# Fewer operations in a 64-bit weight conversion, row gates on ScalarE, output weights split in pieces, and a last pair of products by row tiles

## The chip, the core and the metric

The kernel runs on one core of a Trainium2 chip. Five engines work side by side, each through its own instructions in order: TensorE (PE, matrix products), VectorE (DVE), ScalarE (ACT), GpSimd (POOL) and SyncE (SP, which issues most transfers). They meet through semaphores. The metric is the device time of one execution in microseconds (us), lower is better: here the median of three executions.

## The reference, cut to what matters

Three layers follow each other; the input is 4 batches of 768 positions, 8 heads of 64, so 3072 tokens of 512 numbers.

```python
x = attention(q, k, v)            # 8 global positions, a local window of 96, per-head distance bias
logits = x @ moe_w_gate;  e = argmax(logits);  gate = softmax(logits)[e]
y[t] = gate[t] * (relu(x[t] @ w1[e[t]]) @ w2[e[t]])        # 8 experts, 512 -> 1024 -> 512
out = (sigmoid(y @ w_gate) * (y @ w_val)) @ w_out          # 512 -> 1536 -> 512, weights are float64
```

The three weights of the last layer arrive as 64-bit floats; everything else is 32-bit. The output is 32-bit.

## The kernel before, in words

**Values split in two.** Products run in 16-bit floats at full rate. A 32-bit value becomes a high half (`wh`, `xh`, `hh`) and a low half, value minus high (`wl`, `xl`, `hl`), and a product becomes three: high-high, high-low, low-high. High halves are copies on ScalarE; low halves are subtractions on VectorE.

**Stage 1, to about 215 us: attention**, laid out by a planner. The change does not touch it.

**Stage 2, about 215 to 524 us: the experts** (`ffn`). Tokens are gathered by expert; the experts are ranked by load and make nine items with 256, 256, 480, 448, 416, 400, 384, 368 and 352 token columns. Each item has eight steps `f`, written out one after the other. In a step TensorE does the 12 products of `mm1` for the step to come (tile `hp`), and the 12 of `mm2` for this one (tiles `acc`). ScalarE makes `hh` from `hp`, VectorE makes `hl`. Beside that, a step prepares what comes later:

- `wsplit`: ScalarE's `wh` and VectorE's `wl` (128x1024) of the weights of the step to come;
- for `f` from 1 to 4, `xgate` on a gathered row tile of the next item: VectorE multiplies 128x512 numbers by the token's gate, one number per row (tile `xg`). Two steps later `xprep` turns `xg` on TensorE and splits it into `xT`. The row tile `x` came by GpSimd's indirect transfer;
- the class `Prep` converts the 64-bit weights in 36 pieces of 128x512, up to six pieces an item. `start` reads the two 32-bit words (`raw`): ScalarE takes the absolute value of the high word as a float (L926, `u`), VectorE shifts the low word (L927, `v`), scales and bounds `u` (L928), joins the two (L929), and puts the sign back (L936). A step later `finish` stores the result or, for the output weights, which come in pairs, forms four differences on GpSimd (L960). A step after that it splits the pair into 16-bit halves (`parts`): a block of 256 columns and one of 1536, each a copy on ScalarE (L946) and a subtraction on GpSimd (L947). One step later SyncE stores them (L950, memory `wz`). Six pairs are done so, one an item; the splits stand in the step `f` = 2 and the store in `f` = 3, one step later in the last of these items.

**Stage 3, about 524 to 1035 us: the gated layer** (`Gated`), in four chunks of 768 tokens. `first` makes the hidden values `h` by seven products in place of eight (sums and differences of blocks stand in for one product). `second` multiplies by the output weights, again seven products a chunk (numbers 0 to 6), each of 54 matmuls on 256 columns. For each, `hsplit` makes the two halves of a block of `h` (tile `wk`, two buffers), `hsum` the next sum of blocks, and `post` adds results to the output tiles `o`, whose rows are sent by GpSimd's indirect transfers (`scatter`, L1494). Every product has two of the eight PSUM banks: X is 6 and 7, Z 4 and 5, W 2 and 3, Y 0 and 1, in the order X, Z, X, W, Y, Z, W. Product 6 thus writes banks that `post` of 4 reads. In the last chunk product 6 goes row tile by row tile into banks 2, 3 and 0. Just ahead of it stand range checks and a `vote`, a 128x2 product on TensorE of VectorE's verdicts (`ok`), from which a flag chooses at the end whether a slower general path must run.

The order on each engine is the order in which the code is written; a tile waits for its buffer.

## Time and profile before

| | us |
|---|---|
| time, three runs | 1037.35, 1037.74, 1038.54; median 1037.74 |
| the profiled execution | 1036.72, of which span 1034.9 |
| attention, experts, gated layer | to about 215, to about 524, to the end |
| TensorE busy | 93% of the span, mean granted clock 0.986 of full |

A group of rows below is one view of this profiled execution: busy time by engine, waits by who was waited for, or the timeline of an engine, in which square brackets hold the idle time before an instruction and what ended it. Line numbers are those of the kernel above.

### The profile page before, as it was taken

How to read it: one execution, taken by the hardware profiler on the slowest of the kernel's cores; microseconds unless marked ns; L12 is line 12 of the kernel's file. 1: busy time of each engine (PE TensorE's matmuls, PEld its weight loads, DVE VectorE, ACT ScalarE, POOL GpSimd, SP SyncE). 2: the span in 40 equal slices, each digit the busy share in tenths (PEclk: the TensorE clock that was granted, in tenths of full speed). 3: DMA queues.
4: the chain of work that ended last, by engine and by line, in shares of the span. 5: the costliest groups of instructions: out<-in, count | busy, mean ns of one | idle time of the engine just before them, and what ended most of it. 6: DMA issues, size and time to landing. Idle time of an engine off the chain costs nothing. (4 is left out here: it accounts for less than half of the span.)

```text
span 1034.9 us, 21115 instructions
## 1 busy us (share of the span) xinstructions
PE 962.7 (93%) x7983; PEld 674.3 (65%) x7983; DVE 780.9 (75%) x1628; ACT 502.4 (49%) x960; POOL 443.5 (43%) x617
## 2 busy tenths in 40 slices
PE   6989887799999999998999999999999999999994
PEld 4778776678555555565555578666786668766684
DVE  5989988975789899988776789444884449744594
ACT  5989888743445545554644354212532226221340
POOL 7799988951412512423567840323112250222102
PEclk9999999989999999999999999999999999999998
DMA  9677676257887998896668646453164523554031
GB/s 198 165 183 181 160 166 144 75 169 239 257 295 252 309 310 269 296 317 222 177 204 284 217 146 235 166 200 133 62 230 172 204 98 118 209 201 175 1 123 65
DMA packets 165701, 197.35 MB, mean 191 GB/s; under 512 B 88547, under 2 KB 129910, under 8 KB 165590
## 3 DMA queue, kind: packets, MB, share of 16 engines
q1 hardware_dynamic: 159990, 181.73, 55.9%
q0 software_dynamic: 5008, 14.11, 4.1%
q8 instruction: 64, 1.05, 0.4%
q14 instruction: 47, 0.39, 0.1%
q10 hardware_dynamic: 592, 0.08, 0.1%
HBM read 146.81 MB, written 49.23 MB: 189 GB/s over the span
## 5 line engine op out<-in xcount | busy, mean ns | idle before, releaser
L1351 PE MATMUL q<-yo,set 128*128 128x384 f16 x2016 | 330.5, 326 | 2.1 <-DVE h L1398 1.8
L1351 PEld LDWEIGHTS <-set 128*128 128x128 f16 x2016 | 197.1, 98 | 134.3 <-issue 5.1
L1442 PE MATMUL p<-wy,wk 128*128 128x256 f16 x1458 | 160.5, 273 | 2.0 <-DVE wk L1338 2.0
L1442 PEld LDWEIGHTS <-wk 128*128 128x128 f16 x1512 | 147.5, 98 | 20.6 <-DVE wk L1338 3.1
L1121 PE MATMUL hp<-xT,wh 128*128 128x256 f16 (+7 forms) x576 | 135.9, 323 | 0.3
L1402 POOL TENSOR_TENSOR h<-h,t 128x384 f32<-128x384 f32 x60 | 59.0, 997 | 151.9 <-DVE t L1398 136.4
L1121 PE MATMUL hp<-xT,wl 128*128 128x256 f16 (+7 forms) x288 | 93.1, 323 | 9.4 <-DVE wl L1022 9.4
L1494 POOL DMA_INDIRECT out_dram<-o,idt x24 | 23.5, 980 | 181.5 <-DVE o L1458 174.1
L1022 DVE SCALAR_TENSOR_TENSOR wl<-wr,wh 128x1024 f16<-128x1024 f32 x64 | 95.3, 1490 | 7.1 <-ACT wh L1017 6.3
L1138 PE MATMUL acc<-hl,wh 128*128 128x256 f16 (+7 forms) x288 | 92.8, 322 | 5.6 <-DVE hl L1126 5.6
L1372 ACT ACTIVATE u<-q 128x384 f32<-128x384 f32 x48 | 23.1, 481 | 153.9 <-PE q L1351 153.9
L1138 PE MATMUL acc<-hh,wh 128*128 128x256 f16 (+7 forms) x288 | 93.0, 323 | 0.0
L1138 PE MATMUL acc<-hh,wl 128*128 128x256 f16 (+7 forms) x288 | 92.7, 322 | 0.0
L1036 POOL DMA_INDIRECT x<-xd,idx x29 | 33.1, 1140 | 129.9 <-DMA idx<-lst 123.2
L1404 ACT ACTIVATE h<-h 128x384 f32<-128x384 f32 x72 | 37.6, 522 | 102.3 <-DVE h L1398 72.5
L570 ACT ACTIVATE pp<-tt,mall 128x232 f32<-128x232 f32 (+1 forms) x192 | 81.5, 487 | 5.1 <-DVE mall L553 3.4
L1125 ACT ACTIVATE hh<-hp 128x256 f16<-128x256 f32 (+7 forms) x72 | 34.6, 480 | 99.2 <-PE hp L1121 97.8
L1138 PEld LDWEIGHTS <-wh 128*128 128x128 f16 x576 | 56.4, 98 | 35.2 <-issue 0.7
L1374 DVE TENSOR_TENSOR u<-q,u 128x384 f32<-128x384 f32 x48 | 26.8, 558 | 68.0 <-PE q L1351 68.0
L1121 PEld LDWEIGHTS <-wh 128*128 128x128 f16 x576 | 56.4, 98 | 31.3 <-ACT wh L1017 0.5
L553 DVE CUSTOM_DVE_ANT_0 tt<-s,nb 128x232 f32<-128x232 f32 (+1 forms) x192 | 64.5, 365 | 0.3 <-PE s L541 0.3
L1017 ACT ACTIVATE wh<-wr 128x1024 f16<-128x1024 f32 x60 | 62.9, 1049 | 3.1 <-DMA wr<-in_moe_w_dram 3.1
(214 smaller groups left out, 1929.9 us busy)
## 6 DMA issues: line engine op xcount, KB each, us to landing
wr<-in_moe_w_dram SPq DMA_DIRECT2D x64, 512.0 KB, 5.7
set<-us SPq DMA_DIRECT2D x36, 896.0 KB, 4.8
wy<-wz SPq DMA_DIRECT2D x28, 768.0 KB, 4.4
us<-set SPq DMA_DIRECT2D x12, 896.0 KB, 6.1
kn<-in_k_dram SPq DMA_DIRECT2D x24, 256.0 KB, 4.9
qn<-in_q_dram SPq DMA_DIRECT2D x24, 256.0 KB, 5.3
vn<-in_v_dram SPq DMA_DIRECT2D x24, 256.0 KB, 4.7
raw<-in_moe_w_gate_dram SPq DMA_DIRECT2D x12, 512.0 KB, 5.7
```

What stands on the lines that cost most here:

```text
L553: nc.vector.tensor_tensor_reduce(out=tt[s][:, j, :w], in0=S_[s][j % 2][:, j // 2, :w], in1=g.nb[w][:, h, :], scale=-0.125 / (QSC * QSC), s ...
L570: nc.scalar.activation(pp[s][:, j, 256 - w :], tt[s][:, j, :w], AF.Exp, bias=g.mall[:, t, h : h + 1], scale=-1.0)
L1017: self.tc.nc.scalar.activation(hi, raw, AF.Copy, scale=WS[z])
L1022: self.tc.nc.vector.scalar_tensor_tensor(lo, self.raws.pop((z, p)), WS[z], hi, op0=ALU.mult, op1=ALU.subtract)
L1036: self.tc.nc.gpsimd.indirect_dma_start(out=x, out_offset=None, in_=self.g.xd[0:n], in_offset=bass.IndirectOffsetOnAxis(ap=self.idx[i][:, j ...
L1121: nc.tensor.matmul(bk, a[:, k, fs], b[:, k, :], start=(m == 0), stop=(m == 11))
L1125: nc.scalar.activation(hh, bk, AF.Relu)
L1138: nc.tensor.matmul(acc[i][dk], a[:, f % 2, d], b, start=(f == 0 and m == 0), stop=(f == NF - 1 and m == 2))
L1351: nc.tensor.matmul(bk, w[:, za, a, us], self.y[zy][:, y, u, :], start=(start and n == 0), stop=(n == 5), skip_group_check=not start,)
L1402: (V if last else G).tensor_tensor(at(half, tok), at(half, tok), d, op=ALU.mult)
L1404: A.activation(d, d, AF.Sigmoid, scale=1.0 / (YS * AS[0]))
L1442: nc.tensor.matmul(bks[t], w[:, za, j, 128 * t : 128 * t + 128], y[:, j, zy, :], start=(new and j == 0 and m == 0 and (end or t != 1)), st ...
```

## The change

- The bound on small numbers goes from the conversion, and the scale moves into ScalarE's absolute value, so L928 has no successor; shift and join stay, with another join (`or`).
- `xgate` runs on ScalarE for all items but the first: 27 of 29 tiles.
- The pair's split comes in four pieces, 256, 512, 512 and 512 columns, one a step, at `f` = 2 to 5, with the store at `f` = 6; in the last of these items at 3 to 6 and 7.
- `wk` has three buffers. In `second`'s loop the next `hsplit` and `hsum` now stand ahead of `post`.
- In the last chunk products 5 and 6 go together, row tile by row tile (`close`), into the banks 4 and 2, 5 and 3, 6 and 0; results are added and scattered tile by tile. The vote is cut in three: verdicts after the second of the six groups, the product ahead of the fifth, the flag after it.

```diff
 KEPT = (0, 2, 3, 4, 5, 6, 7)
-W64MIN = float(1.125 * 2.0 ** -15)
+EXP8 = 2.0 ** -112
...
@@ -923,10 +923,9 @@
         u = g.cv.tile([128, 512], U32, tag="u", name="u", bufs=3)
         v = g.cv.tile([128, 512], U32, tag="v", name="v", bufs=1)
         uf = u.bitcast(F32)
-        nc.scalar.activation(uf, hi.bitcast(F32), AF.Abs)
-        nc.vector.tensor_scalar(v, lo, 29, 0x80000000, op0=ALU.logical_shift_right, op1=ALU.bitwise_or)
-        nc.vector.tensor_scalar(uf, uf, W64MIN, 2.0 ** -16 * (OX if m == 2 else 1.0), op0=ALU.max, op1=ALU.mult)
-        nc.vector.scalar_tensor_tensor(u, u, 3, v, op0=ALU.logical_shift_left, op1=ALU.bitwise_xor)
+        nc.scalar.activation(uf, hi.bitcast(F32), AF.Abs, scale=EXP8 * (OX if m == 2 else 1.0))
+        nc.vector.tensor_single_scalar(v, lo, 29, op=ALU.logical_shift_right)
+        nc.vector.scalar_tensor_tensor(u, u, 3, v, op0=ALU.logical_shift_left, op1=ALU.bitwise_or)
         if m == 2:
             if f < NJ:
                 self.pair = g.cv.tile([128, 8, 256], U32, tag="pair", name="pair", bufs=2)
@@ -939,15 +938,7 @@
     def finish(self):
         g, nc = self.g, self.tc.nc
         if self.late:
-            j, x, z = self.late.pop(0)
-            if z is None:
-                z = g.cv.tile([128, len(KEPT), 2, 256], F16, tag="parts", name="parts", bufs=2)
-                for o, b, k in ((0, 0, 1), (1, 2, 6)):
-                    nc.scalar.activation(z[:, o : o + k, 0, :], x[:, b : b + k, :], AF.Copy)
-                    nc.gpsimd.tensor_tensor(z[:, o : o + k, 1, :], x[:, b : b + k, :], z[:, o : o + k, 0, :], op=ALU.subtract)
-                self.late.append((j, x, z))
-            else:
-                nc.sync.dma_start(out=g.wz[:, :, j].rearrange("b p z c -> p b (z c)"), in_=z.rearrange("p b z c -> p b (z c)"))
+            self.late.pop(0)()
         if self.half is None:
             return
         f, m, uf = self.half
@@ -958,7 +949,19 @@
             x = self.pair.bitcast(F32)
             for o, a, b in ((4, 1, 0), (6, 3, 1), (5, 3, 4), (7, 2, 5)):
                 nc.gpsimd.tensor_tensor(x[:, o, :], x[:, a, :], x[:, b, :], op=ALU.subtract)
-            self.late.append((f - NJ, x, None))
+            z = g.cv.tile([128, len(KEPT), 2, 256], F16, tag="parts", name="parts", bufs=2)
+            def split(o, b, k):
+                hi, lo = (z[:, o : o + k, y, :] for y in range(2))
+                nc.scalar.activation(hi, x[:, b : b + k, :], AF.Copy)
+                nc.gpsimd.tensor_tensor(lo, x[:, b : b + k, :], hi, op=ALU.subtract)
+            def store():
+                nc.sync.dma_start(
+                    out=g.wz[:, :, f - NJ].rearrange("b p z c -> p b (z c)"), in_=z.rearrange("p b z c -> p b (z c)")
+                )
+            self.late += [lambda a=a: split(*a) for a in ((0, 0, 1), (1, 2, 2), (3, 4, 2), (5, 6, 2))] + [store]
...
         x = self.rows.pop((i, j))
         y = self.xg[i, j] = self.mr[0].tile([128, DM], F32, tag="xg", name="xg")
-        self.tc.nc.vector.tensor_scalar(y, x[:, 0:DM], x[:, DM : DM + 1], None, op0=ALU.mult)
+        if i == 0:
+            self.tc.nc.vector.tensor_scalar(y, x[:, 0:DM], x[:, DM : DM + 1], None, op0=ALU.mult)
+        else:
+            self.tc.nc.scalar.activation(y, x[:, 0:DM], AF.Copy, scale=x[:, DM : DM + 1])
     def xturn(self, i, j, b):
...
         left = lambda n, bufs: ctx.enter_context(tc.tile_pool(name=n, bufs=bufs, reuse_waits="tile"))
-        self.raw_p, self.set_p, self.wk_p, self.tm = left("raw2", 2), left("set2", 4), left("wk2", 2), left("tm2", 1)
+        self.raw_p, self.set_p, self.wk_p, self.tm = left("raw2", 2), left("set2", 4), left("wk2", 3), left("tm2", 1)
         yo = left("yo2", 1)
...
@@ -1424,26 +1430,55 @@
         nc = self.tc.nc
         w, y = self.wk.pop(n), self.wy.pop(n)
         k = "XZXWYZW"[n]
-        new, end = n != 2, c == NCH - 1 and n == len(ORDER) - 1
-        if end:
-            self.acc["E"] = [self.psum(b, f"e{b}")[:, 0:256] for b in (2, 3, 0)]
-        elif new:
+        new = n != 2
+        if new:
             lo, hi = (self.psum(i, f"p{i}") for i in {"X": (6, 7), "Z": (4, 5), "W": (2, 3), "Y": (0, 1)}[k])
             self.acc[k] = lo.rearrange("p (t d) -> p t d", t=2), hi[:, 0:256].rearrange("p (t d) -> p t d", t=1)
-        steps = [(j, t) for j in range(NJ) for t in range(NH)]
-        if end:
-            steps.sort(key=lambda x: x[1])
-            bks = self.acc["E"]
-        else:
-            lo, hi = self.acc[k]
-            bks = [lo[:, 0, :], lo[:, 1, :], hi[:, 0, :]]
-        for j, t in steps:
-            for m, (za, zy) in enumerate(((0, 0), (0, 1), (1, 0))):
-                nc.tensor.matmul(
-                    bks[t], w[:, za, j, 128 * t : 128 * t + 128], y[:, j, zy, :],
-                    start=(new and j == 0 and m == 0 and (end or t != 1)), stop=(j == NJ - 1 and m == 2),
-                    skip_group_check=not end,
-                )
+        lo, hi = self.acc[k]
+        bks = [lo[:, 0, :], lo[:, 1, :], hi[:, 0, :]]
+        for j in range(NJ):
+            for t in range(NH):
+                for m, (za, zy) in enumerate(((0, 0), (0, 1), (1, 0))):
+                    nc.tensor.matmul(
+                        bks[t], w[:, za, j, 128 * t : 128 * t + 128], y[:, j, zy, :],
+                        start=(new and j == 0 and m == 0 and t != 1), stop=(j == NJ - 1 and m == 2),
+                        skip_group_check=True,
+                    )
+    def close(self, c, check):
+        nc = self.tc.nc
+        V = nc.vector
+        n = len(ORDER) - 1
+        sides = [(self.wk.pop(n + z), self.wy.pop(n + z)) for z in (-1, 0)]
+        r = slice(256, DM)
+        k = 1.0 / (HS * OS * H4)
+        for t in range(NH):
+            bks = []
+            for z, (w, y) in enumerate(sides):
+                b = ((4, 2), (5, 3), (6, 0))[t][z]
+                bk = self.psum(b, f"e{b}")[:, 0:256]
+                if (t, z) == (NH - 1, 0):
+                    self.vote[1]()
+                for j in range(NJ):
+                    for m, (za, zy) in enumerate(((0, 0), (0, 1), (1, 0))):
+                        nc.tensor.matmul(
+                            bk, w[:, za, j, 128 * t : 128 * t + 128], y[:, j, zy, :],
+                            start=(j == 0 and m == 0), stop=(j == NJ - 1 and m == 2),
+                        )
+                bks.append(bk)
+                o = self.o[1 - z]
+                V.scalar_tensor_tensor(o[:, t, r], bk, k, o[:, t, r], op0=ALU.mult, op1=ALU.add)
+                self.scatter(c, 1 - z, t)
+                if z == 0:
+                    V.scalar_tensor_tensor(self.o[0][:, t, r], bk, k, self.u[:, t], op0=ALU.mult, op1=ALU.add)
+                if (t, z) == (0, 1):
+                    check(4)
+                    self.vote[0]()
+                if (t, z) == (NH - 1, 0):
+                    self.vote[2]()
+        last = self.psum(7, "last")
+        nc.tensor.matmul(last[:, 0:1], self.g.ident, self.o[0][:, NH - 1, DM - 1 : DM], start=True, stop=True)
     def post(self, c, n):
         V, A = self.tc.nc.vector, self.tc.nc.scalar
...
             each(add, "Z", o[0][:, :, r], u)
-        elif n == 6 and c == NCH - 1:
-            for t, bk in enumerate(self.acc["E"]):
-                add(bk, o[0][:, t, r], o[0][:, t, r])
-                self.scatter(c, 0, t)
...
-                if n:
-                    self.post(c, n - 1)
                 if n < last:
                     for j in (0, 3):
                         self.hsplit(n + 1, j, j + 3)
                     if n < 4:
                         for j in (0, 3):
                             self.hsum((3, 5, 4, 6)[n], j, j + 3)
+                if n:
+                    self.post(c, n - 1)
                 self.second(c, n)
                 if n + 3 <= last:
                     self.oload(n + 3)
@@ -1555,14 +1586,18 @@
                     if n in (2, 3, 4):
                         self.afetch(s + n - 2)
                 if not more and n == 0:
-                    check, vote = verdict(tc, g)
+                    check, self.vote = verdict(tc, g)
                 if not more and n < 4:
                     check(n)
-                if not more and n == 5:
-                    check(4)
+                if not more and n == last - 2:
+                    self.hsplit(last, 0, 3)
+                    self.hsplit(last, 3, NJ)
+                    self.post(c, n)
                     check(5)
-                    vote()
-            self.post(c, last)
+                    self.close(c, check)
+                    break
+            else:
...
-    def vote():
...
+    def gather():
...
+    def sums():
...
+        nc.tensor.matmul(held[0][:, 0:2], g.ones16, ok16, start=True, stop=True)
...
+    def count():
...
+    vote = gather, sums, count
```

**ScalarE**, from the second to the fourth step of the 400-column item. `u` is a conversion's first operation, `wh` a weight's high half, `parts` a split, `xT` a turned token tile. Before:

```order
L1017 ACTIVATE wh_7560<-wr_7371 128x1024
L1125 ACTIVATE hh<-hp 128x400
L926 ACTIVATE u<-raw 128x512
L1017 ACTIVATE wh_7610<-wr_7434 128x1024
L946 ACTIVATE parts<-pair 128x256
L946 ACTIVATE parts<-pair 128x6x256
L1125 ACTIVATE hh<-hp 128x400
L926 ACTIVATE u<-raw 128x512
L1067 ACTIVATE xT_7662<-mxt 128x4x128
L1017 ACTIVATE wh_7671<-wr_7475 128x1024
L1125 ACTIVATE hh<-hp 128x400
```

And now, in the same place:

```order
L1020 ACTIVATE wh_7550<-wr_7360 128x1024
L1053 ACTIVATE xg<-x 128x512
L1131 ACTIVATE hh<-hp 128x400
L926 ACTIVATE u<-raw 128x512
L1020 ACTIVATE wh_7600<-wr_7424 128x1024
L1053 ACTIVATE xg<-x 128x512
L956 ACTIVATE parts<-pair 128x256
L1131 ACTIVATE hh<-hp 128x400
L926 ACTIVATE u<-raw 128x512
L1073 ACTIVATE xT_7648<-mxt 128x4x128
L1020 ACTIVATE wh_7657<-wr_7466 128x1024
L1053 ACTIVATE xg<-x 128x512
```

One gate a step has come in ahead of `hh`, and the large split is in pieces, of which the next 512 columns follow the last row shown.

**VectorE**, chunk 0 of the second loop, at products 5 and 6. `yo` belongs to the chunk to come, `u` and `o` are `post` of 4, `wk` is the split for product 6 at its second place. Before:

```order
L1338 SCALAR_TENSOR_TENSOR wk_10179<-h_9060,wk_10179 128x1152 x2
L1271 TENSOR_TENSOR yo_8703<-raw_9794,yo_8702 128x3x384
L1458 SCALAR_TENSOR_TENSOR u<-p_10184,u 128x512
L1458 SCALAR_TENSOR_TENSOR u<-p_10185,u 128x256
L1458 SCALAR_TENSOR_TENSOR o_9968<-p_10117,u 128x2x256
L1458 SCALAR_TENSOR_TENSOR o_9968<-p_10118,u 128x256
L1474 TENSOR_TENSOR o_9968<-o_9968 128x3x256
L1475 COPY oc<-o_9968 128x3
L1338 SCALAR_TENSOR_TENSOR wk_10250<-h_9060,wk_10250 128x1152 x2
```

And now:

```order
L1344 SCALAR_TENSOR_TENSOR wk_10167<-h_9048,wk_10167 128x1152 x2
L1277 TENSOR_TENSOR yo_8691<-raw_9782,yo_8690 128x3x384
L1344 SCALAR_TENSOR_TENSOR wk_10232<-h_9048,wk_10232 128x1152 x2
L1493 SCALAR_TENSOR_TENSOR u<-p_10172,u 128x512
L1493 SCALAR_TENSOR_TENSOR u<-p_10173,u 128x256
L1493 SCALAR_TENSOR_TENSOR o_9963<-p_10105,u 128x2x256
L1493 SCALAR_TENSOR_TENSOR o_9963<-p_10106,u 128x256
L1509 TENSOR_TENSOR o_9963<-o_9963 128x3x256
L1510 COPY oc<-o_9963 128x3
```

The split for product 6 has moved ahead of `post` of 4, which now reads banks 2 and 3 (`p_10105`, `p_10106`) behind it.

**VectorE**, the last operations before the flag is read. `e` are the banks of the row tiles, `bad`, `most` and `flag` are the vote's count. Before:

```order
L1606 TENSOR_TENSOR flag<-bad,most 128x1
L1458 SCALAR_TENSOR_TENSOR o_13676<-p_13961,o_13676 128x2x256
L1458 SCALAR_TENSOR_TENSOR o_13676<-p_13962,o_13676 128x256
L1458 SCALAR_TENSOR_TENSOR o_13675<-p_13961,u 128x2x256
L1458 SCALAR_TENSOR_TENSOR o_13675<-p_13962,u 128x256
L1458 SCALAR_TENSOR_TENSOR o_13675<-e_14057,o_13675 128x256
L1458 SCALAR_TENSOR_TENSOR o_13675<-e_14058,o_13675 128x256
L1458 SCALAR_TENSOR_TENSOR o_13675<-e_14059,o_13675 128x256
```

And now:

```order
L1471 SCALAR_TENSOR_TENSOR o_13674<-e_14016,o_13674 128x256
L1474 SCALAR_TENSOR_TENSOR o_13673<-e_14016,u 128x256
L1471 SCALAR_TENSOR_TENSOR o_13673<-e_14040,o_13673 128x256
L1471 SCALAR_TENSOR_TENSOR o_13674<-e_14063,o_13674 128x256
L1474 SCALAR_TENSOR_TENSOR o_13673<-e_14063,u 128x256
L1643 TENSOR_SCALAR bad<-vote 128x1
L1644 TENSOR_TENSOR most<-bad,most 128x1
L1645 TENSOR_SCALAR bad<-vote 128x1
L1647 TENSOR_TENSOR flag<-bad,most 128x1
L1471 SCALAR_TENSOR_TENSOR o_13673<-e_14094,o_13673 128x256
```

The six groups are read one by one as they end, and only one addition stands behind the count.

## Rows read from the trace of the kernel before

**Rows 1.** The page, part 1: busy time, share, instructions

```profile
PE 962.7 (93%) x7983; PEld 674.3 (65%) x7983; DVE 780.9 (75%) x1628; ACT 502.4 (49%) x960; POOL 443.5 (43%) x617
```

**Rows 2.** Waits of TensorE from 250 to 1035 us: total, times, longest

```profile
PE hp L1121 <- DVE wl L1022: 9.4, 7, 2.4
PE acc L1138 <- DVE hl L1126: 5.4, 4, 2.4
...
PE p L1442 <- DVE wk L1338: 2.0, 4, 0.8
```

**Rows 3.** Timeline of TensorE: start, us, engine, line, out<-in, [idle before <-releaser]

```profile
258.80 0.27 PE L1138 MATMUL acc<-hl,wh 128*128 128x256 f16 x1 [1.37 <-DVE hl L1126]
...
262.99 0.27 PE L1138 MATMUL acc<-hl,wh 128*128 128x256 f16 x1 [0.97 <-DVE hl L1126]
...
399.90 0.34 PE L1121 MATMUL hp<-xT,wl 128*128 128x400 f16 x1 [2.01 <-DVE wl L1022]
...
436.18 0.34 PE L1121 MATMUL hp<-xT,wl 128*128 128x384 f16 x1 [2.38 <-DVE wl L1022]
...
510.07 0.31 PE L1138 MATMUL acc<-hl,wh 128*128 128x352 f16 x1 [0.71 <-DVE hl L1126]
...
513.41 0.32 PE L1121 MATMUL hp<-xT,wl 128*128 128x352 f16 x1 [0.94 <-DVE wl L1022]
```

**Rows 4.** Timeline of VectorE and GpSimd around 395 us

```profile
395.72 4.12 DVE L1022 SCALAR_TENSOR_TENSOR wl<-wr,wh 128x1024 f16<-128x1024 f32 x1
...
395.31 3.45 POOL L947 TENSOR_TENSOR parts<-pair,parts 128x1536 f16<-128x1536 f32 x1 [0.78 <-ACT parts L946]
```

**Rows 5.** Single lines of the kernel: duration ns minimum/median/maximum

```profile
L928 DVE TENSOR_SCALAR u<-u x36: 411/419/949, 251.0 to 478.4; 128x512 f32<-128x512 f32 x36
...
L1022 DVE SCALAR_TENSOR_TENSOR wl<-wr,wh x64: 1210/1216/4132, 201.6 to 515.1; 128x1024 f16<-128x1024 f32 x64
...
L1047 DVE TENSOR_SCALAR xg<-x x29: 470/479/3332, 208.6 to 477.3; 128x512 f32<-128x512 f32 x29
...
L926 ACT ACTIVATE u<-raw x36: 655/672/694, 250.3 to 473.3; 128x512 f32<-128x512 f32 x36
...
L606 POOL TENSOR_TENSOR pl<-pf,ph x23: 660/1154/1167, 19.8 to 202.5; 128x512 f16<-128x512 f32 x19, 128x256 f16<-128x256 f32 x4
```

**Rows 6.** Windows: length, busy of each engine, granted clock, DMA share, GB/s

```profile
350.00:400.00 50.00, 46.36 (x273) 26.74 (x272) 46.93 (x64) 27.99 (x42) 19.06 (x14) 1.00 0.88 291
436.80:440.20 3.40, 3.40 (x13) 1.67 (x11) 3.33 (x7) 1.04 (x2) 0.00 (x0) 0.50 0.23 85
414.00:418.00 4.00, 4.00 (x25) 2.21 (x24) 3.86 (x8) 2.48 (x4) 1.56 (x1) 1.00 1.05 387
```

**Rows 7.** Timelines of VectorE and TensorE, second loop, chunk 0

```profile
640.76 1.01 DVE L1458 SCALAR_TENSOR_TENSOR u<-p,u 128x512 f32<-128x512 f32 x2
...
643.80 2.62 DVE L1338 SCALAR_TENSOR_TENSOR wk<-h,wk 128x1152 f16<-128x1152 f32 x2
...
645.21 4.98 PE L1442 MATMUL p<-wy,wk 128*128 128x256 f16 x44 [0.79 <-DVE wk L1338]
```

**Rows 8.** Timeline of several engines, end of the program

```profile
1009.65 1.02 DVE L1458 SCALAR_TENSOR_TENSOR u<-p,u 128x512 f32<-128x512 f32 x2 [1.44 <-PE p L1442]
...
1017.16 0.18 PE L1596 MATMUL vote<-ok,ones 128*128 128x2 f16 x1 [1.32 <-DVE ok L1594]
...
1017.20 6.05 PE L1442 MATMUL e<-wy,wk 128*128 128x256 f16 x54
...
1018.03 1.01 DVE L1458 SCALAR_TENSOR_TENSOR o<-p,o 128x512 f32<-128x512 f32 x2
...
1019.48 1.01 POOL L1494 DMA_INDIRECT out_dram<-o,idt  x1 [50.86 <-DVE o L1458]
...
1023.29 0.42 DVE L1458 SCALAR_TENSOR_TENSOR o<-e,o 128x256 f32<-128x256 f32 x1 [1.54 <-PE e L1442]
...
1025.89 0.97 POOL L1494 DMA_INDIRECT out_dram<-o,idt  x1 [0.30 <-issue]
```

More of the change, by code (lines that the diff above doesn't have):

```diff
@@ L1557, in run @@
                 if not more and n == 0:
[L1558 removed]
+                    check, self.vote = verdict(tc, g)
                 if not more and n < 4:
                     check(n)
[L1561 to L1562 removed]
+                if not more and n == last - 2:
+                    self.hsplit(last, 0, 3)
+                    self.hsplit(last, 3, NJ)
+                    self.post(c, n)
                     check(5)
[L1564 to L1565 removed]
+                    self.close(c, check)
+                    break
+            else:
+                self.post(c, last)
 def verdict(tc, g):
@@ L1585, in check @@
         nc.vector.tensor_reduce(ok[:, i : i + 1], a, axis=AX.X, op=ALU.min)
-    def vote():
-        ok16 = p.tile([128, 2], F16, name="ok16", bufs=1)
+    ok16 = p.tile([128, 2], F16, name="ok16", bufs=1)
+    most = p.tile([128, 1], F32, name="most", bufs=1)
+    bad = p.tile([128, 1], F32, name="bad", bufs=1)
+    held = []
+    def gather():
         nc.vector.tensor_reduce(ok16[:, 0:1], ok, axis=AX.X, op=ALU.min)
@@ L1594, in vote @@
         nc.vector.tensor_single_scalar(ok16[:, 1:2], big, OUTMIN * OUTMIN, op=ALU.is_ge)
-        bk = g.ps.tile([128, 512], F32, tag="b1", name="vote")
-        nc.tensor.matmul(bk[:, 0:2], g.ones16, ok16, start=True, stop=True)
         over = p.tile([128, E], F32, name="over", bufs=1)
-        most = p.tile([128, 1], F32, name="most", bufs=1)
-        bad = p.tile([128, 1], F32, name="bad", bufs=1)
         nc.vector.tensor_tensor(over, g.nr, g.capv, op=ALU.is_gt)
         nc.vector.tensor_reduce(most, over, axis=AX.X, op=ALU.max)
-        nc.vector.tensor_scalar(bad, bk[:, 0:1], 127.5, 2.0, op0=ALU.is_lt, op1=ALU.mult)
+    def sums():
+        held.append(g.ps.tile([128, 512], F32, tag="b1", name="vote"))
+        nc.tensor.matmul(held[0][:, 0:2], g.ones16, ok16, start=True, stop=True)
+    def count():
+        nc.vector.tensor_scalar(bad, held[0][:, 0:1], 127.5, 2.0, op0=ALU.is_lt, op1=ALU.mult)
         nc.vector.tensor_tensor(most, bad, most, op=ALU.max)
-        nc.vector.tensor_scalar(bad, bk[:, 1:2], 0.5, 2.0, op0=ALU.is_lt, op1=ALU.mult)
+        nc.vector.tensor_scalar(bad, held[0][:, 1:2], 0.5, 2.0, op0=ALU.is_lt, op1=ALU.mult)
         g.flag = g.const.tile([128, 1], I32, name="flag")
         nc.vector.tensor_tensor(g.flag, bad, most, op=ALU.max)
+    vote = gather, sums, count
     return check, vote
```

6 lines of the change are left out of this document (3 added, 3 removed).

## Prediction

> **What bounds the kernel now.** I read the busy shares first. TensorE is busy for 93% of the span, VectorE for 75%, ScalarE for 49% [rows 1], so what a change can win is mostly the time in which TensorE stands. The waits by who was waited for come next: in the expert stage TensorE waits 9.4 us for VectorE's `wl` and 5.4 us for its `hl`, together 14.8; in the second loop 2.0 us for `wk` [rows 2], and once 1.3 us for the vote [rows 8]. The timeline then says where the 14.8 lie [rows 3]: 1.37 and 0.97 in the second 256-column item; 0.71 and 0.94 in the last item; the other 10.8 (14.8 less 2.34 less 1.65) in the items of 448 to 368 columns, mostly as one wait of up to 2.38 us an item.
>
> Why there: `wl` takes 1.22 us in the median but 4.12 at 395.72 [rows 4, 5]. GpSimd began its 1536-column subtraction of the split at 395.31 and ended at 398.76; `wl` ended 1.1 us behind that. So VectorE stood for 2.9 us (4.12 less 1.22) beside one GpSimd operation, and the matmul at 399.90 waited 2.01 us for it. VectorE has nothing to give: from 350 to 400 us it is busy for 46.93 of 50 us, where TensorE has 46.36 [rows 6]. With 273 matmuls in that window and 26 a step in the mean (24 products, and four transposes in half of the steps), a step is 4.8 us (26/273 of 50), of which VectorE has 0.3 idle.
>
> **The change part by part.** Sums are against the profiled execution, 1036.72 us (span 1034.9 and 1.8 around it); the median of the three runs is 1.0 higher.
>
> *A, VectorE's load and the split.* Off VectorE go 36 operations of 0.42 us (L928) and 27 gates of 0.48 [rows 5]: 15.1 and 13.0 us, or 0.9 us in a step that has both. The subtraction of 3.45 us becomes three of 512 columns, in three steps. The same form elsewhere, L606, took 1.15 [rows 5]. If VectorE again stands for as long as GpSimd works, a step loses 1.15 us rather than 2.9. In the step that waited, VectorE is relieved of 1.75 + 0.9 = 2.65 us, more than the longest wait, 2.38. The two steps behind it get 1.15 where they had nothing, against 0.3 idle and 0.9 removed: just even. I leave 0.25 us of wait for each of six items, 1.5, for that tightness. In the 256-column item VectorE loses two L928 and two or three gates, some 2 us, ahead of the two waits (2.34 us). A conversion there still begins only when its raw words land, so I leave 0.4. The last item converts nothing, and I leave its 1.65. A = 14.8 - 1.5 - 0.4 - 1.65 = 11.3 us. Its ends: 14.8, if all goes, and 1.9, if only the 256-column item gains (the first rival).
>
> What it puts on ScalarE: a gate there has no row. The nearest are L926, 0.67 us for 128x512 floats [rows 5], and, at the low end, VectorE's own 0.48; I take 0.67, and twice that as the high end, since the gate reads a number for each row. A split's 1536-column copy becomes three, at about L926's price each. ScalarE is busy 27.99 of 50 us [rows 6], 2.7 a step; one gate and one 512-column copy make it 4.0 of 4.8. It fits; `hh` in that step comes up to 1.3 us later, and its readers, `hl` and the second product, stand a product of 12 matmuls (half a step, 2.4 us) behind. That is the cover. Were it gone, 0.67 us a gate would show.
>
> The Trainium skill speaks against this move: "ScalarE: Activation LUTs", section "Rules for kernel authors", sends multiplications to VectorE rather than ScalarE. The rows agree as to the single operation (0.67 on ScalarE for the same tile, 0.48 on VectorE), but here the first has 22 us free of 50 and the second 3. The same page, section "What ACT_TABLE_LOAD costs", puts 0.09 us on an operand with a number for each row; by that a gate would be an estimated 0.76, and the sum the same as long as the cover holds.
>
> The differences of a pair on GpSimd (L960) and all matmuls stay as they are. SyncE issues the same transfers; the store of a pair (896 KB) is three steps later, and in the last converting item stands directly ahead of the first loads of the gated layer (third rival). GpSimd's gathers now wait for ScalarE to have read the row buffer rather than VectorE; they are issued two steps behind the last gate, which covers it.
>
> *B, the clock.* Right behind the 2.38 us wait at 436.18, the granted clock from 436.8 to 440.2 is 0.50, the lower of the two levels, 1.2 GHz [rows 3, 6]. TensorE had stood idle just ahead of it. 3.4 us at half speed lose 1.7. If the wait goes, so does this: B = 1.7, ends 0 and 1.7.
>
> *C, the second loop.* A third buffer lets ScalarE and VectorE start a split earlier; I give it nothing, since around these products VectorE goes from one operation into the next and has no time for which an earlier start would help. What moves is order: the split for product 6, 2.62 us, goes ahead of `post` of 4 (two pairs of 1.01) [rows 7]. Its wait of 0.79 goes, but `post` then reads banks 2 and 3 late, and product 6 writes them. In chunk 0: split from 640.76 to 643.3, reading to 644.9 or 645.2, TensorE there at 644.4 (645.21 less 0.79): a new wait of about 0.5. In the next two chunks, where the old wait was shorter, I put 0.1 and 0; the fourth of the old waits, for product 5, about 0.5, stays. That leaves 1.1 of 2.0: C = 0.9, ends -1.0 (a full 1.01 read on the path behind the split once more in two chunks, less what is won) and 2.0.
>
> *D, the end.* TensorE's wait of 1.32 at 1017.16 was for the checks behind the split [rows 8]. Now the split for 6 can run as soon as VectorE is free, at 1008.2 (1009.65 less its idle 1.44), to 1010.8. `post` of 4 has then read `u` at 1011.8 and bank 2 some 0.4 later. The first group of `close` ends at about 1011.7 (1009.7 and 2.0, a third of 6.05), and the second, which writes bank 2, waits some 0.4; the vote's verdicts are done two groups before they are needed. So TensorE ends 0.9 earlier. The scatters: the last addition ends at 1023.71 (1023.29 and 0.42), but the last scatter starts at 1025.89, 2.18 later, since six of 1.27 us (0.97 and 0.30 of issue) queue; the first started 0.44 behind its addition (1019.48 less 1019.04) [rows 8]. Now there is one scatter a group of 18 matmuls, 2.0 us, so none queues: 1.75 us. D = 2.65; ends 0.9, if a queue stays, and 3.5, if both go whole. The 128x1 matmul that is new at the end lies beside the scatters.
>
> Sum: 11.3 + 1.7 + 0.9 + 2.65 = 16.6. 1036.7 - 16.6 = 1020.1, and with the 1.0 between the profiled run and the median **1021.1 us**.
>
> **The rivals.**
>
> *Pieces hold VectorE just as much.* Three times 1.15 is 3.45, as before. If a GpSimd piece under VectorE's load takes 1.8 rather than 1.15 us, each of 18 steps is short by 0.6 (1.8 less the 1.2 that it has), 10.8 us: all the waits of the middle items come back. Left are 1.9 + 0.9 + 2.65 = 5.5: 1032.2. For it: VectorE is as full as TensorE. Against: 19 of L606's operations are within 1.17 us, beside a VectorE at work too. The Trainium skill ("GPSIMD Engine Reference", section 1, "Specifications") has GpSimd share its SBUF interfaces with VectorE, contending with VectorE's operations of two SBUF inputs; the 4.12 us agree, and by that rule the total stand would stay at 3.45 an item, spread out.
>
> *ScalarE becomes the bound (slower).* Its queue is in order: a gate stands ahead of `hh`, and waits there for its gather. If the 2.4 us of cover are used up, every gate lands on TensorE, 27 times 0.67, 18.1 us, against 16.6 won: 1039.2. It decides from a delay of `hh` above 2.4 us a step. Against: ScalarE is busy for 56% there [rows 6].
>
> *Transfers.* From 414 to 418 us the transfers are at a share of 1.05 and 387 GB/s [rows 6]; freed of VectorE, TensorE asks for weights sooner, and the last store goes ahead of the gated layer's loads: 896 KB at 291 GB/s are 3.1 us; with a like wait for weights once more, 4: 1025.
>
> **How the numbers follow.** Forecast 0.74, transfers 0.12, pieces 0.09, ScalarE 0.05. The best ends (14.4, 1.7, 2.0, 3.5) give 21.6, 1016.1; the forecast with A at 7 and C at 0 is near 1026. The range is 1016 to 1028, which leaves out the pieces' and ScalarE's cases and little else. This kernel's runs tell 0.2%, 2.1 us, from no change: all but ScalarE's case and some of the worst of the others are faster by more, 0.93; same 0.03; slower 0.04.
>
> **What would show it.** A: no `wl` above about 2.4 us, GpSimd's split in pieces of about 1.15, TensorE's waits for `wl` and `hl` near 3.5 rather than 14.8; ScalarE some 4 us busy in steps 3 to 5. B: no granted clock of 0.50 between 250 and 520 us. C: a wait of a product for `post` near product 6. D: last scatter within 0.6 us of the last addition. Wrong, if TensorE waits for `hh` or a DMA in the experts, or if `wl` is still stretched by 2.9 us.

## The result, and the profile after

The median went from 1037.74 to 1023.56 us (four runs from 1021.74 to 1023.99); the ratio is 0.9859, its interval 0.9842 to 0.9876. The forecast was 1021.1 in a range of 1016 to 1028. The profiled execution after took 1023.99, with a span of 1022.1.

TensorE's waits from 250 to 1035 us answer to [rows 2] (total, times, longest):

```profile
PE hp L1127 <- DVE wl L1025: 2.8, 4, 1.1
PE q L1357 <- DVE h L1404: 1.8, 6, 0.5
PE acc L1144 <- DVE hl L1132: 1.7, 2, 1.0
PE p L1442 <- PE p L1442: 1.2, 3, 0.6
PE acc L1144 <- ACT hh L1131: 1.2, 1, 1.2
```

The 14.8 us for `wl` and `hl` are 4.5, and a wait for ScalarE's `hh` is new. The timeline of TensorE in the expert stage (as [rows 3]) says where the remaining waits are:

```profile
259.26 0.27 PE L1144 MATMUL acc<-hl,wh 128*128 128x256 f16 x1 [0.71 <-DVE hl L1132]
...
433.33 0.34 PE L1127 MATMUL hp<-xT,wl 128*128 128x384 f16 x1 [0.32 <-DVE wl L1025]
...
466.22 0.33 PE L1127 MATMUL hp<-xT,wl 128*128 128x368 f16 x1 [1.11 <-DVE wl L1025]
...
488.67 0.32 PE L1127 MATMUL hp<-xT,wl 128*128 128x352 f16 x1 [0.41 <-DVE wl L1025]
...
495.07 0.31 PE L1144 MATMUL acc<-hh,wh 128*128 128x352 f16 x1 [1.16 <-ACT hh L1131]
...
496.42 0.31 PE L1144 MATMUL acc<-hl,wh 128*128 128x352 f16 x1 [1.03 <-DVE hl L1132]
...
500.59 0.47 PE L1127 MATMUL hp<-xT,wl 128*128 128x352 f16 x1 [0.91 <-DVE wl L1025]
```

The middle items, 10.8 us before, have 1.43 left. The last item, which converts nothing, went from 1.65 to 3.51. Windows (as [rows 6]: length, busy of PE, PEld, DVE, ACT, POOL, granted clock, DMA share, GB/s):

```profile
350.00:400.00 50.00, 50.00 (x302) 29.89 (x301) 43.00 (x60) 32.22 (x54) 18.11 (x16) 1.00 0.95 305
497.50:504.50 7.00, 6.03 (x22) 2.61 (x21) 6.06 (x6) 4.45 (x8) 5.11 (x4) 0.52 0.15 42
```

Where TensorE had 273 matmuls in 50 us it has 302 and stands no more; VectorE has 7 us free rather than 3. But the low clock, gone at 436 us, is back in the last item: 1.2 GHz behind the waits at 495 and 496. Single lines (as [rows 5]):

```profile
L1025 DVE SCALAR_TENSOR_TENSOR wl<-wr,wh x64: 1202/1226/3171, 198.9 to 502.3; 128x1024 f16<-128x1024 f32 x64
...
L1053 ACT ACTIVATE xg<-x x27: 706/712/727, 232.1 to 459.6; 128x512 f32<-128x512 f32 x27
...
L957 POOL TENSOR_TENSOR parts<-pair,parts x24: 836/1160/1871, 274.8 to 470.0; 128x512 f16<-128x512 f32 x18, 128x256 f16<-128x256 f32 x6
```

A gate takes 0.71 us on ScalarE (0.67 was taken), a piece on GpSimd 1.16 in the median (1.15 was taken), though eight of the 18 large ones take 1.5 to 1.9. The longest `wl`, 3.17 us, is no part of this: it is the first, at 198.87 us, ahead of the experts, and it has 3.17 us in every profile of this record. Beside a piece the longest `wl` is 2.11 us, where it was 4.13. The Trainium skill, "ScalarE: Activation LUTs", section "What ACT_TABLE_LOAD costs", gives 280 ns and 0.833 ns an element for an operation with such an operand: an estimated 0.71 for 512, which these rows bear out better than the 0.76 that the prediction pieced together.

**The ledger of the two profiled executions.** "Low clock" is the time by which matmuls at 1.2 GHz stand further apart than their like at 2.4, summed; waits here include those under 0.3 us and the stage from its first matmul. Where the text gives the waits of one item, they are those of 0.3 us and more.

| stretch | before | after | won | forecast |
|---|---|---|---|---|
| start to first expert matmul | 216.8 | 214.7 | 2.1 | 0 |
| expert stage | 307.4 | 298.5 | 8.9 | 13.0 (A, B) |
| of it TensorE's waits | 15.3 | 6.0 | 9.3 | 11.3 |
| of it low clock | 1.7 | 2.4 | -0.7 | 1.7 |
| to the first output product | 83.8 | 84.0 | -0.1 | 0 |
| from there to the last addition | 415.7 | 413.8 | 1.9 | } 3.55 |
| last addition to the end | 11.2 | 11.2 | 0.0 | } (C, D) |

### The profile page after: what moved, and what is told of

Same layout as the page of the kernel before. It is cut to its first block, busy times and chain, and to the rows that moved or that the text cites. A ratio compares the mean times of both kernels' runs of the same rounds, so it can differ in the third digit from the quotient of the medians.

```text
span 1022.1 us, 21110 instructions
## 1 busy us (share of the span) xinstructions
PE 960.4 (94%) x7985; PEld 673.4 (66%) x7985; DVE 743.5 (73%) x1567; ACT 517.0 (51%) x999; POOL 449.7 (44%) x629
## 4 chain that ended last, share of the span: by engine, by line
PE 48%; issue 2%; DVE 2%; DMA 2%; ACT 1%; SPq 0%; POOL 0%; POOLq 0%; DVEq 0%
PE q L1357 29%; PE p L1442 15%; PE hp L1127 1%; PE e L1465 1%; PE acc L1144 1%; DMA raw<-in_moe_w_gate_dram 1%; DMA wr<-in_moe_w_dram 1%; DVE wl L1025 0%; DMA yT<-y 0%; DVE h L1404 0%; DVE h L1390 0%; ACT wh L1020 0%; DVE u L928 0%; SPq L1261 0%; DVE xT L1077 0%
## 5 line engine op out<-in xcount | busy, mean ns | idle before, releaser
L1442 PE MATMUL p<-wy,wk 128*128 128x256 f16 x1404 | 154.4, 273 | 1.2 <-PE p L1442 1.2
L1442 PEld LDWEIGHTS <-wk 128*128 128x128 f16 x1404 | 137.1, 98 | 18.3 <-issue 2.0
L1025 DVE SCALAR_TENSOR_TENSOR wl<-wr,wh 128x1024 f16<-128x1024 f32 x64 | 85.8, 1342 | 17.3 <-ACT wh L1020 17.1
L1132 DVE SCALAR_TENSOR_TENSOR hl<-hp,hh 128x256 f16<-128x256 f32 (+7 forms) x72 | 39.0, 543 | 39.8 <-ACT hh L1131 39.6
L957 POOL TENSOR_TENSOR parts<-pair,parts 128x512 f16<-128x512 f32 (+1 forms) x24 | 32.0, 1334 | 75.1 <-ACT parts L956 75.1
```

What stands on the lines that cost most here:

```text
L957: nc.gpsimd.tensor_tensor(lo, x[:, b : b + k, :], hi, op=ALU.subtract)
L1025: self.tc.nc.vector.scalar_tensor_tensor(lo, self.raws.pop((z, p)), WS[z], hi, op0=ALU.mult, op1=ALU.subtract)
L1132: nc.vector.scalar_tensor_tensor(hl, bk, 0.0, hh, op0=ALU.max, op1=ALU.subtract)
L1442: nc.tensor.matmul(bks[t], w[:, za, j, 128 * t : 128 * t + 128], y[:, j, zy, :], start=(new and j == 0 and m == 0 and t != 1), stop=(j == ...
```

## The experiments

Three groups of four, each group on one chip with its own runs of the kernel before, whose median was 1041.6, 1036.8 and 1037.5; only ratios compare across groups. On these chips single runs of a kernel scatter by up to 9 us or so, so I read the stages in the profiles beside the ratios. In the first group every profile has one more wait, of 2.3 to 2.7 us in two parts, at about 239 us. Expert stage, waits and low clock are in us.

| run | ratio to before, interval | expert stage | waits | low clock |
|---|---|---|---|---|
| after_again | 0.9843, 0.9811 to 0.9875 | 297.3 | 6.2 | 1.6 |
| store_earlier | 0.9863, 0.9827 to 0.9900 | 299.4 | 8.2 | 1.3 |
| before_store_late | 1.0004, 0.9985 to 1.0024 | 313.1 | 19.2 | 3.1 |
| pieces_only | 0.9972, 0.9949 to 0.9995 | 311.2 | 17.1 | 3.2 |
| store_by_piece | 0.9852, 0.9829 to 0.9875 | 296.6 | 6.7 | 0 |
| convert_only | 0.9915, 0.9896 to 0.9934 | 300.7 | 10.4 | 0 |
| gates_only | 0.9968, 0.9953 to 0.9983 | 304.0 | 10.5 | 3.3 |
| before_three_scatters | 1.0018, 1.0005 to 1.0030 | 311.3 | 14.8 | 6.4 |
| store_earlier_b | 0.9857, 0.9835 to 0.9879 | 295.2 | 4.2 | 1.3 |
| undo_pieces | 0.9899, 0.9883 to 0.9915 | 296.2 | 6.4 | 0 |
| close_only | 0.9984, 0.9969 to 0.9999 | 307.9 | 14.6 | 2.9 |
| order_only | 0.9985, 0.9973 to 0.9998 | 310.4 | 16.5 | 3.4 |

### What relieved VectorE

**convert_only**: before, with `start` of the changed kernel.

```diff
-        nc.vector.tensor_scalar(uf, uf, W64MIN, 2.0 ** -16 * (OX if m == 2 else 1.0), op0=ALU.max, op1=ALU.mult)
+        nc.scalar.activation(uf, hi.bitcast(F32), AF.Abs, scale=EXP8 * (OX if m == 2 else 1.0))
...
```

> The kernel before, with only the shorter conversion (36 operations of 0.42 us off VectorE). Theory (VectorE is full and stands 2.9 us once an item): wl still up to 4.13 us, but each long wait of TensorE 0.4 to 0.8 shorter, the two in the 256-column item half: waits 14.8 to about 10, time 5 lower. Rival (only the stand counts): waits 14, time within 1 us.

**gates_only**: before, with `xgate` of the changed kernel.

```diff
-        self.tc.nc.vector.tensor_scalar(y, x[:, 0:DM], x[:, DM : DM + 1], None, op0=ALU.mult)
...
+            self.tc.nc.scalar.activation(y, x[:, 0:DM], AF.Copy, scale=x[:, DM : DM + 1])
```

> The kernel before, with only the 27 gates on ScalarE. Theory: VectorE gets 0.48 us back in steps 1 to 4 of an item, waits 14.8 to about 10, a gate takes about 0.67 on ScalarE and hh is not late: time 4 to 5 lower. Rival (ScalarE becomes the bound): TensorE waits for hh or wh, time up to 18 higher.

**pieces_only**: before, with the split in pieces; the last pair is split in three steps rather than four, as in store_earlier below.

```diff
-                for o, b, k in ((0, 0, 1), (1, 2, 6)):
...
+                self.late += [lambda a=a: split(*a) for a in ((0, 0, 1), (1, 2, 2), (3, 4, 2), (5, 6, 2))] + [store]
```

> The kernel before, with only the split in pieces (the last pair's store one step ahead of the loads, as in the run with the earlier store). Theory (VectorE stands as long as one GpSimd operation runs): wl at most 2.6 us rather than 4.13, the waits of the items of 448 to 368 columns fall from 10.8 to about 5, the fall of the clock at 436 us goes: 1030 to 1033. Rival (pieces hold VectorE just as much in all): the waits stay near 10, 1036 to 1038.

The waits of TensorE from 250 to 530 us, of convert_only, then gates_only, then pieces_only:

```profile
PE acc L1138 <- DVE hl L1126: 5.1, 6, 1.9
PE hp L1121 <- DVE wl L1022: 4.3, 5, 1.2
```

```profile
PE hp L1124 <- DVE wl L1022: 7.1, 5, 2.6
PE acc L1141 <- DVE hl L1129: 2.5, 4, 1.0
```

```profile
PE acc L1145 <- DVE hl L1133: 6.7, 5, 2.5
PE hp L1128 <- DVE wl L1029: 6.4, 7, 2.0
```

Conversion and gates are each worth what was expected in waits: 15.3 to 10.4 and 10.5. The conversion's 8.8 us in time is more than that, the gates' 3.3 less; the conversion's profile has no low clock, gates_only's has 3.3 us of it. One expectation failed: in convert_only `wl` is not "still up to 4.13", beside a split it takes at most 1.70. The large block of GpSimd is as long as before, but in convert_only it meets `xg` in all six items (3.32 to 3.33 us each), in gates_only the conversion's shift `v` in five (2.15 to 2.93) and `wl` in one (4.12); before it met `wl` in five of six. So these runs do not part the time saved on VectorE from the place where the stand falls. In gates_only TensorE waited for no `hh`; the one `wh` it waited for (0.7 us) comes in the last item, where convert_only has it too. ScalarE is not the bound, and that rival falls.

The pieces alone save little: 13.1 us remain of 14.8, and the time is 2.9 us lower, with an interval from 0.5 to 5.3. That is the rival of the prediction that pieces hold VectorE as much in all, and alone it nearly holds. `wl` is indeed at most 1.94 us beside a piece (2.6 was expected), but other operations stand instead. Two rows of pieces_only, VectorE and GpSimd at 441 us, and the next wait of TensorE:

```profile
441.93 1.30 DVE L927 TENSOR_SCALAR v<-raw 128x512 uint32<-128x512 uint32 x1
...
441.80 1.16 POOL L958 TENSOR_TENSOR parts<-pair,parts 128x512 f16<-128x512 f32 x1 [1.73 <-ACT parts L957]
```

```profile
446.81 0.34 PE L1128 MATMUL hp<-xT,wl 128*128 128x384 f16 x1 [2.04 <-DVE wl L1029]
```

The conversion's shift, 0.42 us as a rule, stands through the piece. A VectorE without idle time hands each such delay on to the next `wl`.

How much VectorE stands can be summed over all splits: the time by which its operations beside GpSimd's subtractions exceed the shortest of their like (differences of 0.1 us and more). It is 21.1 us before, 20.4 in convert_only, 16.8 in gates_only, 17.0 in pieces_only, but 7.9 and 6.5 in the two profiles of the changed kernel. There most pieces begin while a `wl` already runs and go on beside `hl`, which reads `hp` from PSUM and which no split stretched by more than 0.02 us in any of these profiles. VectorE, then GpSimd, in the changed kernel:

```profile
358.97 0.59 DVE L1132 SCALAR_TENSOR_TENSOR hl<-hp,hh 128x416 f16<-128x416 f32 x1 [0.31 <-ACT hh L1131]
359.48 0.57 DVE L927 TENSOR_SCALAR v<-raw 128x512 uint32<-128x512 uint32 x1
```

```profile
358.61 1.16 POOL L957 TENSOR_TENSOR parts<-pair,parts 128x512 f16<-128x512 f32 x1 [5.64 <-ACT parts L956]
```

**undo_pieces**: the changed kernel, with `finish` of the kernel before (the store is early again too).

```diff
-            self.late += [lambda a=a: split(*a) for a in ((0, 0, 1), (1, 2, 2), (3, 4, 2), (5, 6, 2))] + [store]
+                for o, b, k in ((0, 0, 1), (1, 2, 6)):
```

> The changed kernel with the split undone: 256 and 1536 columns in one step and the store early, as in the kernel before. Theory of the prediction (the pieces are what ends the long waits): wl again at 4.1 us, a wait of about 1 us in each of five items, expert-stage waits 9 to 10, the time 3 to 5 us over the changed kernel's. Rival (the relief of VectorE by conversion and gates is what counts, as those two runs alone suggest: 15.3 less 4.9 less 4.8): waits 5.6, and with the store early the time is equal or 2 us lower.

VectorE, then GpSimd, at 424 us in undo_pieces:

```profile
424.66 2.88 DVE L927 TENSOR_SCALAR v<-raw 128x512 uint32<-128x512 uint32 x1
```

```profile
423.45 3.79 POOL L946 TENSOR_TENSOR parts<-pair,parts 128x1536 f16<-128x1536 f32 x1 [0.26 <-ACT parts L945]
```

In the profile the rival is right: waits 6.4, near its 5.6, with the block back. VectorE is early enough by then that the stand meets a conversion's shift in all six items (2.03 to 2.88 us), for which nobody waits at once; `wl` takes at most 1.70 us beside a split (4.1 was expected), TensorE's longest wait is 1.98. VectorE's stand is 15.3 us in all, twice that of the changed kernel, and this execution absorbs it. The time says something else: 0.9899, where the changed kernel had 0.9859 and 0.9843 and store_earlier_b, in the same group, 0.9857: 4 to 6 us slower, about the 3 to 5 expected of the pieces. One profile against five runs can't settle it. That the other executions lost more to the low clock would fit: the mean granted clock is 0.988 in the profiled run, the fastest of the five, and 0.981 to 0.985 in the others. But the two fastest runs of store_earlier_b have 0.985 as well, and no profile shows where these lost it. The pieces' share stays open between 0 and 6 us.

### The last item: SyncE's queue

The two profiles after agree that the last item waits longer than in the profile before, and SyncE's queue shows one way. After, VectorE's last part of the results `y` and SyncE:

```profile
477.26 0.54 DVE L1154 TENSOR_SCALAR y<-acc 128x368 f32<-128x368 f32 x1 [0.39 <-PE acc L1144]
```

```profile
471.74 0.37 SPq L960 DMA_DIRECT2D wz<-parts  x1
472.22 0.50 SPq L1261 DMA_DIRECT2D raw<-yT  x1
472.77 1.13 SPq L1262 DMA_DIRECT2D raw<-yT  x1
473.95 0.85 SPq L1263 DMA_DIRECT2D raw<-yT  x1
480.06 0.41 SPq L1155 DMA_DIRECT2D yT<-y  x1
...
484.53 1.55 SPq L1261 DMA_DIRECT2D raw<-yT  x1
...
487.23 1.54 SPq L1011 DMA_DIRECT2D wr<-in_moe_w_dram  x3
```

The results are ready at 477.80 and go out at 480.06, because the loads of `yT` (472.2 to 474.8), behind the 896 KB of `wz`, have to land first; the next loads wait for that store, and the last weights (487.23) stand behind them. Before, the same lag was 0.13 us (ready 493.68, issued 493.81). The transfers were near full while those loads ran, and nearly idle while the store stood waiting (length, busy of PE, PEld, DVE, ACT, POOL, clock, DMA share, GB/s):

```profile
472.00:478.00 6.00, 6.00 (x42) 3.86 (x40) 3.29 (x5) 3.30 (x6) 0.00 (x0) 1.00 0.92 297
478.00:480.00 2.00, 2.00 (x15) 1.33 (x14) 1.68 (x2) 1.16 (x3) 0.79 (x1) 1.00 0.06 19
```

ScalarE waits for the last weights, and its `hh` stands behind their copy; that is TensorE's wait for `hh` at 495.07. The last gate is at 459.6, well ahead of it:

```profile
493.61 1.06 ACT L1020 ACTIVATE wh<-wr 128x1024 f16<-128x1024 f32 x1 [4.85 <-DMA wr<-in_moe_w_dram]
494.58 0.45 ACT L1131 ACTIVATE hh<-hp 128x352 f16<-128x352 f32 x1
```

The lag is not all of it. In the seven profiles with a lag of at most 0.3 us the last item waits between 1.5 and 2.9 us, and 1.65, the profile before, is the second lowest. These waits rise in step with the time from the issue of those last weights to ScalarE's copy, from 5.5 to 6.5 us. Where that time is 5.4 to 5.8 us, three profiles with a lag of 1.5 us and more wait 2.5 to 2.9, three with a short one 1.5 to 2.2. So I estimate the lag at about 1 us; in the profiled pair that time also went from 5.7 to 6.4.

**after_again**: the changed kernel, unchanged.

> The changed kernel once more, so that the others of this group have its time and profile beside them: 1021.7 to 1024. If the 2.1 us by which its attention ended earlier than before's were the change, they come again; if they are scatter between executions, attention ends anywhere within some 2 us.

Its lag is 2.6 us, its last item waits 2.8 us and loses 1.6 us to the low clock. Its attention ends at 214.7; over all fourteen profiles, of kernels with the same attention, that is 213.9 to 216.8. So the 2.1 us of the ledger are scatter.

**before_store_late**: before, with the last pair's store three steps later.

```diff
+                if j == NJ - 1:
+                    self.late = [None, None, None] + self.late
```

> The kernel before, with only the last pair's store moved three steps on, to directly ahead of the gated layer's first loads. Theory (SyncE's queue): the last item loses 2 us of waits and, if the clock falls as well, 3.5 more: 1040 to 1043. Rival (the delay comes with the faster experts): no change, 1037.7.

No change in time. The lag rose to 0.9 us, the last item waited 2.9 us; before_three_scatters, with the store early and a lag of 0.6, has the same 2.9, and order_only, with a lag of 0.1, has 2.8. The rival is right here: the late store alone costs nothing that can be measured.

**store_earlier**, **store_earlier_b** and **store_by_piece**: the changed kernel, with other cuts for the last pair.

```diff
+                self.late += [lambda a=a: [split(*x) for x in a] for a in (((0, 0, 1), (1, 2, 2)), ((3, 4, 2),), ((5, 6, 2),))] + [store]
...
+                self.late += [lambda a=a: [split(*x) for x in a] for a in (cuts[:1], cuts[1:2], cuts[2:])] + [store]
...
+                    self.late.append(lambda i=i, a=a: (i and store(cuts[i - 1][0], cuts[i - 1][2]), split(*a)))
```

> The changed kernel, with the last pair split in three steps rather than four (256 and 512 columns in the first), so that its store is issued one step ahead of the gated layer's first loads rather than directly ahead of them. Theory (SyncE's queue: the store of 896 KB delays those loads, the store of the seventh expert's results waits behind them, and with it the last expert's weights): the results' store goes out within 0.5 us of the results rather than 2.2 us later, TensorE's waits in the last item fall from 3.5 to about 1.7 us, no granted clock of 0.50 there, 1018.5 to 1019.5. Rival (the last weights are late because the transfers are full): same waits, 1023.5.

> The changed kernel, with the last pair split as 256, 512 and then twice 512 columns in one step, where no conversion runs any more, and its store one step earlier. Theory: the seventh results' store goes out within 0.6 us of the results, and without the 2.83 us wait that the run with 256 and 512 columns in the first step had: expert stage about 294 us against 297 to 298.5 of the changed kernel, waits about 5, no fall of the clock; time 3 us under the changed kernel's, near 1018 to 1020 where before is 1037. Rival (four splits are needed one a step): a wait of 2 us or more for wl or hl behind the double split, no gain.

> The changed kernel, with the last pair's store cut into its four pieces, each sent one step after its split: 256 KB rather than 896 KB stand directly ahead of the gated layer's first loads, and the split stays one piece a step. Theory (SyncE's queue and the 896 KB): the seventh results go out within 0.6 us of being ready rather than 2.2 later, TensorE's waits in the last item fall from about 3 to about 1.7 us, the clock holds there: expert stage 4 us shorter than the changed kernel's beside it, time 3 to 5 lower, near 1019 on a chip where the changed kernel takes 1023.5. Rival (the transfers are full, the order does not matter): no change.

In store_earlier the lag is 0.3 us, the last item waits 1.5 us and keeps the full clock, as the theory has it (its last weights also came in 5.5 us, among the fastest); but TensorE stood at 471.77 and lost the gain:

```profile
471.77 0.49 PE L1130 MATMUL hp<-xT,wl 128*128 128x368 f16 x1 [2.83 <-DVE wl L1028]
```

In store_earlier_b no wait came behind the double split, but the store waited on SyncE for GpSimd until 471.01 and again stood right ahead of the loads (lag 2.9): the last item waited 2.9 us and lost 1.3 to the low clock. In store_by_piece the lag is 1.2, the clock held, the last item still waited 2.9. All three times lie within the intervals of the changed kernel: none beats it measurably. The lag is seen in the queue; the price that was expected of it in the whole time, 3 to 5 us, was not shown.

### The second loop and the end

**order_only**: before, with three buffers and the next split ahead of `post`.

```diff
-                if n:
-                    self.post(c, n - 1)
                 if n < last:
...
+                if n:
+                    self.post(c, n - 1)
```

> The kernel before, with only the third buffer and the next split ahead of post. Theory (term C): waits for wk 2.0 us become about 1.1 us for the banks that post reads; the second loops 0.9 us shorter. Rival (post late costs as much as the split saved): second loops equal within 0.2 us.

Waits of TensorE from 590 us on:

```profile
PE p L1442 <- PE p L1442: 1.5, 3, 0.8
...
PE p L1442 <- DVE wk L1338: 0.5, 1, 0.5
```

The waits for `wk` have become waits for banks (`p` for `p`), 2.0 us as before. In six profiles with the old order the sum is 1.2 to 1.4, in one 2.0; in the seven with the new order it is 1.2 four times, 1.9 twice and 2.0 once. In these waits C is 0, and the rival is right.

But the order has an effect where the prediction did not put C: at the vote. The split for product 6 no longer stands between `post` of 4 and the checks, and TensorE reaches the vote without a wait, where in all six profiles with the old order and the old end it stood 1.32 us:

```profile
1016.59 0.18 PE L1596 MATMUL vote<-ok,ones 128*128 128x2 f16 x1
```

That fits the time of order_only, 1.6 us lower with an interval from 0.2 to 2.8.

**close_only**: before, with `close`, the split vote and three buffers.

```diff
+                if not more and n == last - 2:
...
+                    self.close(c, check)
+                    break
```

> The kernel before, with only the last two products together by row tiles, the vote in three parts and the third buffer. Theory (the end hangs on the last addition): TensorE's 1.3 us for the vote become about 0.5 for bank 2, from the last addition to the end 11.2 us as before: 0.9 us sooner. Rival (term D as predicted, with the transfers' queue on the path): 2.65 us sooner.

**before_three_scatters**: before, without the last chunk's second half of scatters.

```diff
-            self.scatter(c, 1)
+            if c < NCH - 1:
+                self.scatter(c, 1)
```

> The kernel before, without the three transfers of the last chunk's second half (those rows of the output are left out), so that three and not six queue on GpSimd at the end. Theory (the end hangs on the last addition, behind which GpSimd's sequencer goes on while the transfers are worked off): last addition to end 11.2 us as before, no change in time. Rival (my term D: the queue is on the path): 1.7 us sooner.

The end after (as [rows 8]):

```profile
1000.43 4.75 PE L1465 MATMUL e<-wy,wk 128*128 128x256 f16 x42 [0.51 <-PE e L1465]
...
1006.32 0.17 PE L1640 MATMUL vote<-ok,ones 128*128 128x2 f16 x1
...
1009.21 0.97 POOL L1525 DMA_INDIRECT out_dram<-o,idt  x1 [0.99 <-DVE o L1471]
...
1010.48 0.42 DVE L1471 SCALAR_TENSOR_TENSOR o<-e,o 128x256 f32<-128x256 f32 x1 [0.57 <-PE e L1465]
...
1011.67 0.98 POOL L1525 DMA_INDIRECT out_dram<-o,idt  x1 [1.49 <-DVE o L1471]
```

The vote's 1.32 us became 0.51 for bank 2 (0.4 was forecast), and no scatter queues any more: the last starts 0.77 us behind the last addition, where it was 2.18. Yet from the last addition (1010.90) to the end (1022.11) it is 11.21 us, and it was 11.21 before (1023.71 to 1034.92). close_only has 11.20, so its gain lies ahead of it: from the first output product to the last addition it is 413.8 to 414.8 us in the seven profiles with `close` (414.0 in close_only) and 414.4 to 416.7 in the seven without. Of the seven without, two (before_store_late, pieces_only) have their last addition 2.1 us behind its product, by a cause that stays open. The ratio of close_only, 1.6 us, agrees with the 0.9 of the theory and, at its wide interval, does not exclude 2.65. But order_only has as much without `close`, so it is not shown that the row tiles add to what the order gives. Taking three scatters out won nothing either: 1.9 us slower, where 1.7 faster stood for the queue; its 12.7 us behind the last addition hold a gap behind a branch on GpSimd of 2.6 us, where eleven profiles have 0.4 and two kernels with all their scatters 2.6 (gates_only) and 1.7 (undo_pieces). GpSimd's sequencer loads the flag behind the last addition (at 1011.46 after, at 1024.27 before, 0.56 behind it in both) and goes on to its final drain beside the transfers that are still queued: before, that load came 1.6 us ahead of the last scatter's start, and the drain began 3.63 behind the last addition in both. In before_store_late and pieces_only, with the old end, the late last addition found the queue worked off (its scatter started 0.77 behind it), and the end still came 11.3 us behind the addition. The end hangs on the last addition, not on the queue.

## Why the prediction was right, and by what it was off

- **A, right in mechanism.** Of the 10.8 us of the middle items 1.43 are left (1.5 forecast), of the 2.34 of the 256-column item 0.71 (0.4). The relief of VectorE does most of it: conversion and gates take 4.9 and 4.8 us of waits each, in part by moving the stand off `wl`. That the pieces were needed for it is not shown: alone they take at most 2, and their share in the whole is open. The step "VectorE again stands for as long as GpSimd works" was too high for them: in the changed kernel VectorE stands 6.5 to 7.9 us in all, where 18 pieces work for 1.15 to 1.9 us each. No `wl` beside a split is above 2.4, as foretold. As the best end of A the text names 14.8 but adds up 14.4; with 14.8 the best time would be 1015.7 rather than 1016.1.
- **A, the term that was mis-sized**: "The last item converts nothing, and I leave its 1.65." It measured 3.51, and 2.8 again. The third rival had the place, the last store ahead of the gated layer's loads, and a price of 4. The profiles show two things: the lag in SyncE's queue, behind loads that ran in near full transfers (about 1 us by my estimate), and a time of the last weights that differs between executions. The old expert stage had 2.2, 2.8 and 2.9 us in other executions, so 1.65 was a low draw.
- **B, half.** The fall at 436 us went, as its wait did. But falls come behind other waits, and not each time: four executions of the old expert stage (before, before_three_scatters, close_only, order_only), with waits of 14.6 to 16.5 us, lost 1.7, 6.4, 2.9 and 3.4 us. The profiled one had lost least, so the forecast's 1.7 was one draw. The changed one lost 2.4 and 1.6.
- **C, wrong in its place**: 0 rather than 0.9 in the waits that it counted. The wait changed its name, as the text feared, in all chunks. What the order won, 1.3 us at the vote, stood in D.
- **D, its larger part wrong**: "so none queues: 1.75 us". The queue went (last scatter 0.77 us behind the last addition, 0.6 foretold) and gave nothing. The 0.9 of TensorE came (1.32 became 0.51), but the order alone gives it too.
- **ScalarE's rival** fell: a gate at 0.71 us, ScalarE busy 32.2 of 50. Its sign, "TensorE waits for `hh`", did come (1.16 us in the last item), but there ScalarE had waited 4.85 us for weights, and no gate runs that late.
- The sum was 16.6 for 14.2 in the medians, 12.7 in the profiled pair, of which 2.1 is scatter ahead of the stage that changed. Without that luck it is 10.6, and the time would still lie in the range.

## What to carry to other kernels

Where one engine has no idle time, as VectorE here, take work off it before changing what disturbs it: a stand of the same size then meets work for which nobody waits. A transfer moved in an in-order queue has to be priced by what stands behind it, down to the next engine that waits. At a program's end follow each engine's sequencer rather than its last busy row: transfers still being worked off may already be beside the final steps.
